# Bias features by distance, streamed both ways, and a shifted store: a bias prologue of an attention and MoE kernel

## The chip, the cores and the metric

One Trainium2 chip, one core of it. The metric is the device time of one execution in microseconds (us); lower is better. Engines are named as in the profile: PE (TensorE, matmul), PEld (its weight load), DVE (VectorE), ACT (ScalarE), POOL (GpSimd), SP (SyncE, which issues every DMA of this kernel).

## The reference, cut to what matters

Attention with a bias that a small network makes from positions, then two MoE layers. The bias depends on the row i, the column j and the head h, but not on the batch:

```python
scores = scale * np.matmul(q, k.transpose(0, 1, 3, 2))         # B=4, H=8, S=576, D=64
rel = (pos[:, None] - pos[None, :]).astype(np.float32)
psi_rel = np.log1p(np.abs(rel))
psi_i = np.log1p(np.maximum(pos[:, None].astype(np.float32), 1.0))
x = (psi_rel / psi_i)[..., None]
h = np.maximum(x @ w1 + b1, 0.0)                                # 32 hidden
bias = h @ w2                                                   # S x S x H
scores = scores + bias.transpose(2, 0, 1)[None, :, :, :]
# softmax over j, times v; then relu-max MoE (512 -> 768 -> 512), then elu MoE (512 -> 2048 -> 512)
```

Since psi_i is positive, relu(psi_rel/psi_i*w1 + b1)*psi_i = relu(psi_rel*w1 + b1*psi_i): for a row i the feature is a function of the distance |i-j| alone, plus a bias per row.

## The kernel before, in words

The program is one long list of instructions per engine. It begins with a **bias prologue** (lines 121 to 199), goes on to attention (16 units n of two heads of a batch; each unit has five steps c = 0 to 4 of 128 query rows, the last of 64), and ends with the two MoE layers, which are the greater part of the time.

The prologue makes the bias of all 576 rows for all 8 heads, 16 rows at a time, in 36 rounds A. In a round:

- **Features.** Four tiles `f_t` (a4 = 0 to 3), each 128 partitions (4 rows x 32 hidden) x 576 columns, are made from `lw`, the table of log distances times w1 (lines 153 to 167). `lw` has 1148 columns, distance 0 near column 572, and the window of a row starts 4 columns earlier for each tile. A tile is made on ACT (relu with a bias, line 162) or on DVE (maximum, line 165); a small planner chooses, by `BUSY` (what each engine has already) and `COST` (us of one tile).
- **Matmuls.** Each tile is multiplied by `w28` (32 columns) into its own 32 partitions of a PSUM buffer, in two halves of 288 columns (line 183). There are four PSUM buffers (`pb`, `pbb`).
- **Eviction.** PSUM goes to an SBUF tile `o_t` with a scale and a bias per partition: on ACT in rounds 0 to 34 (line 194), on DVE in round 35 (line 192). There are six `o_t` buffers.
- **Store.** SP stores `o_t` to the DRAM scratch `scr` (line 196). After every eighth round SP also loads the two bias tiles of the first pair of heads for chunk c from `scr` (line 109); those loads wait for that chunk's eight stores, and SP is in order, so the next stores stand behind them. Chunk 4 has four rounds and two loads of 64 rows (line 114).

Features run AH = 3 rounds ahead of the matmuls in program order; 18 feature buffers allow four and a half rounds.

Three things of the start matter too. `cst`, the bias of the eviction, needs a small matmul, a copy to `cv` and a multiply (lines 169 to 175); they stand after round 0's matmuls, and the second half of `lw` (line 174) stands there as well. `pk_t`, a pack of small tables, is the first load of SP, and the two halves of `lt_t` come behind it.

Attention's first softmax steps use `ident2`, two 64x64 identities; POOL scales it by the reciprocal row sums into `dg_t` (line 249), and PE transposes the exponentials with that (`flip`, line 252). `ident2` lies in the pool `xp`, which takes over the SBUF of the prologue's feature and `o_t` buffers; the two copies that fill it (lines 210 and 211) stand on DVE behind the first six score instructions (line 230). The score instruction of step c needs the bias tile of chunk c. With n = 0, step c = 4 is the first that needs chunk 4.

## Time and profile before

| what | value |
|---|---|
| median of 3 runs | 1009.87 us (1009.82 to 1012.12) |
| the profiled execution's own time | 1010.22 us |
| its span | 1008.4 us |
| PE busy | 977.4 us, 97% of the span |
| DVE / ACT / POOL busy | 692.1 / 526.1 / 341.7 us |
| mean granted TensorE clock | 0.997 of full speed |

The span is the profiled part of an execution; the execution's own time is 1.8 us longer. A busy share of 97% is a mean over stages: in the prologue, DVE and ACT are busy all the time too, so the stage has to be read by itself. The granted clock is 1.0 where TensorE runs at 2.4 GHz and 0.5 where it runs at 1.2 GHz; a value between them is a stretch with both.

### The profile page before, as it was taken

The page shows a single profiled execution, that of the slowest core. Times are in us where ns is not written, and L with a number is a line of the kernel's source. Part 1 is how long each engine was busy: PE and PEld are TensorE (multiplying, and loading weights), DVE is VectorE, ACT ScalarE, POOL GpSimd, SP SyncE. Part 2 cuts the span into 40 slices and gives each one's busy share as a digit, 9 for nine tenths or more (in the row PEclk, how much of TensorE's full clock was granted, in tenths as well). Part 3 has the DMA queues.
Part 4 walks back from the last instruction along what each step waited for, and adds up shares of the span by engine and source line. Part 5 has one row for each costly group of instructions (what it writes and reads, how often), then busy time and mean ns, then how long its engine had stood idle before and what let it go on. Part 6 is the DMA issues. An engine that isn't in the chain of part 4 may idle for free.

```text
span 1008.4 us, 28525 instructions
## 1 busy us (share of the span) xinstructions
PE 977.4 (97%) x11748; PEld 869.2 (86%) x11748; DVE 692.1 (69%) x1428; ACT 526.1 (52%) x1087; POOL 341.7 (34%) x419
## 2 busy tenths in 40 slices
PE   7979899999999999999999999999999999999998
PEld 4447777778887899999999999998998989988996
DVE  7967778788886699887887862835574355743342
ACT  8967777777775233333333331644445344453443
POOL 0013344344343354534553550323232132321222
PEclk9989999999999999999999999999999999999999
DMA  7842724645532356879886981355657556575553
GB/s 259 291 172 85 247 94 157 205 163 187 176 127 79 134 187 215 308 234 341 321 282 236 328 298 47 116 189 175 199 192 252 191 171 204 188 258 185 176 197 105
DMA packets 65905, 201.00 MB, mean 199 GB/s; under 512 B 7024, under 2 KB 14832, under 8 KB 65776
## 3 DMA queue, kind: packets, MB, share of 16 engines
q1 hardware_dynamic: 65776, 199.18, 57.6%
q8 instruction: 93, 1.52, 0.6%
q14 instruction: 36, 0.29, 0.1%
HBM read 150.78 MB, written 48.37 MB: 197 GB/s over the span
## 4 chain that ended last, share of the span: by engine, by line
PE 91%; DVE 6%; issue 1%; DMA 1%; ACT 0%; SPq 0%; POOL 0%; DVEq 0%; POOLq 0%; ACTq 0%
PE xo L696 18%; PE pb L740 13%; PE pb L526 12%; PE tq L740 6%; PE tq L252 6%; PE xo L319 6%; PE xo L526 5%; PE tq L526 5%; PE pb L222 5%; PE pb L620 4%; PE pb L183 3%; PE pbb L183 2%; DVE e_t L230 2%; PE xo L620 2%; PE tq L620 2%
## 5 line engine op out<-in xcount | busy, mean ns | idle before, releaser
L81 POOL TENSOR_TENSOR gl<-t_t,gh 128x384 fp32r<-128x384 f32 x96 | 108.7, 1142 | 286.3 <-ACT gh L75 286.3
L235 ACT ACTIVATE e_t<-e_t,st_t 128x576 f32<-128x576 f32 x144 | 111.4, 773 | 58.6 <-DVE st_t L240 56.1
L230 DVE CUSTOM_DVE_ANT_0 e_t<-pb,b_t 128x576 f32<-128x576 f32 x144 | 107.7, 749 | 32.7 <-PE pb L222 32.5
L249 POOL TENSOR_SCALAR dg_t<-ident,st_t 128x64 f32<-128x64 f32 x144 | 48.1, 348 | 212.7 <-DVE st_t L241 93.2
L740 PE MATMUL pb<-w_t,gh 128*128 128x512 f32 x384 | 119.3, 392 | 0.0
L526 PE MATMUL pb<-xh,w_t 128*128 128x384 f32 x448 | 116.8, 336 | 0.0
L252 PEld LDWEIGHTS tq<-dg_t,e_t 64*64 64x64 f32 x4608 | 96.6, 136 | 22.7 <-issue 7.7
L252 PE MATMUL tq<-dg_t,e_t 64*64 64x64 f32 x4608 | 97.8, 222 | 10.9 <-issue 5.3
L696 PE MATMUL xo<-tt,w_t 128*128 128x384 f32 x528 | 107.4, 338 | 0.0
L718 ACT ACTIVATE t_t<-c_t 128x384 f32<-128x384 f32 x96 | 50.0, 521 | 103.4 <-DVE c_t L709 95.6
L222 PE MATMUL pb<-kq_t 64*64 64x288 f32 x1152 | 98.6, 413 | 3.8 <-issue 1.3
L696 PEld LDWEIGHTS xo<-tt,w_t 128*128 128x128 f32 x528 | 95.0, 188 | 7.7 <-issue 0.3
L696 PE MATMUL xo<-xh,w_t 128*128 128x384 f32 x328 | 94.6, 335 | 0.0
L319 PE MATMUL xo<-p,tv_t 64*64 64x320 f32 (+1 forms) x1024 | 85.4, 408 | 1.6 <-issue 1.2
L526 PEld LDWEIGHTS pb<-xh,w_t 128*128 128x128 f32 x448 | 81.1, 188 | 0.5 <-issue 0.4
L740 PEld LDWEIGHTS pb<-w_t,gh 128*128 128x128 f32 x384 | 70.5, 188 | 6.6
L740 PE MATMUL pb<-w_t,gl 128*128 128x512 f32 x192 | 75.5, 393 | 0.0
L526 PE MATMUL pb<-xl,w_t 128*128 128x384 f32 x224 | 75.3, 336 | 0.0
L75 ACT ACTIVATE p<-tq 128x512 f32<-128x512 f32 (+1 forms) x128 | 62.8, 528 | 16.4 <-PE tq L252 15.2
L222 PEld LDWEIGHTS pb<-kq_t 64*64 64x64 f32 x1152 | 50.9, 133 | 22.9 <-DVE p L77 4.4
L75 ACT ACTIVATE gh<-t_t 128x384 fp32r<-128x384 f32 x96 | 48.6, 519 | 33.4 <-DVE t_t L726 33.4
L696 PEld LDWEIGHTS xo<-xh,w_t 128*128 128x128 f32 x328 | 60.2, 188 | 3.0
(131 smaller groups left out, 2198.1 us busy)
## 6 DMA issues: line engine op xcount, KB each, us to landing
w_t<-scw_w SPq DMA_DIRECT2D x90, 512.0 KB, 4.4
w_t<-scw_wi SPq DMA_DIRECT2D x74, 512.0 KB, 4.2
kq_t<-tkq SPq DMA_DIRECT2D x16, 864.0 KB, 5.4
scw_wi<-sp SPq DMA_DIRECT2D x26, 512.0 KB, 4.7
scw_w<-sp SPq DMA_DIRECT2D x22, 512.0 KB, 5.5
raw<-wo SPq DMA_DIRECT2D x22, 512.0 KB, 3.7
scr<-o_t SPq DMA_DIRECT2D x36, 288.0 KB, 3.9
raw<-wm SPq DMA_DIRECT2D x18, 512.0 KB, 4.1
```

Of the source, the lines that this page charges most:

```text
L75: nc.scalar.activation(dst, src, AF.Copy)
L81: e.tensor_tensor(out=dst, in0=src, in1=hi.bitcast(F32), op=ALU.subtract)
L183: mm(p[32 * a4:32 * a4 + 32, 224 + 288 * hf:512 + 288 * hf], w28, FT[A, a4][:, 288 * hf:288 * hf + 288], start=True, stop=True)
L222: mm(PB[h][H64[g], 224 + 288 * r:512 + 288 * r], t[H64[r], 576 + 576 * a + q0:640 + 576 * a + q0], t[H64[r], 288 * a:288 * a + 288], start ...
L230: nc.vector.tensor_tensor_reduce(out=E[s][:, 576 * h:576 * h + 576], in0=PB[h][:, 224:800], in1=BT[n // 4, c, h], op0=ALU.add, op1=ALU.min ...
L235: nc.scalar.activation(e, e, AF.Exp, bias=st[:, h:h + 1], scale=-1.0, accum_out=st[:, 2 + h:3 + h])
L252: mm(dst, E[s][H64[g], k0:k0 + 64], DG[s][H64[g], h % nheads(s)], start=True, stop=True)
L319: mm(XO[g][H64[h], 0:w], v[H64[g], 128 * k + 64 * h:128 * k + 64 * h + 64], ps[0][H64[g], 4 * h + k, :], start=(k == 0), stop=(k == 3 and ...
L526: mm(ps[blk][:, 0:NB], wt[:, ks], xt[:, kk, t0:t0 + NB], start=(j == 0), stop=(j == 11))
L620: mm(ps[blk][:, 0:NB], WO[0][:, kk, wt, ms], xt[:, bs], start=(j == 0), stop=(j == 3 * NM1 - 1))
L696: mm(ps, w[wt][:, ks], b[xt][:, kk], start=(start and j == 0), stop=(stop and j == 5), skip_group_check=True)
L740: mm(acc[t], g[:, ts], w[k], start=(f == 0 and i == 0 and j == 0), stop=(f == NU - 1 and i == 1 and j == 2))
```

## The change

- **Features by distance.** `lw` shrinks to 576 columns, one for each distance 0 to 575. A round's features cover only the distances that its 16 rows reach, n = max(576-16A, 16A+16): 576 in round 0, 304 in rounds 17 and 18, 576 again in round 35.
- **Two directions.** The matmuls read a feature tile forwards for the columns j >= i, and backwards (step -1) for those below. A round's PSUM now has 591 columns, the same for all its 16 rows, as if all had the row 16A: two groups of four matmuls in most rounds, three in the first four and the last four, where a PSUM bank's limit splits one direction.
- **Shift on the way to DRAM.** Row i of the 16 is to lie i columns further. The scratch gets rows of 608 floats and the store goes to a start that moves by one float per row, 591 floats of each, so the loads find column 0 at float 16.
- **Order.** The small matmul for `cv` comes ahead of the features; `cv` and `cst` follow round 0's features on DVE. `lt_t` is loaded first, in one piece, then `pk_t`. `ident2` moves to the pool `const` and is filled at the start.
- **Planner.** `BUSY` and `COST` change; `COST` is now a constant and a part for the width. It gives DVE 119 features (51,760 columns, mean 435) and ACT 25 (11,600 columns, mean 464).

```diff
@@ -28,6 +28,7 @@
 NU = NF // 2
 NB = 384
 BIG = 3.0e38
+SW = 608
 
 
 
@@ -45,8 +46,8 @@
 
 EV = "a" * 35 + "v"
 AH = 3
-BUSY = {"v": 4.0, "a": 0.3, "p": 0.0}
-COST = {"v": 0.43, "a": 0.67}
+BUSY = {"v": 0.9, "a": 0.0, "p": 0.0}
+COST = {"v": (0.06, 0.37), "a": (0.26, 0.42)}
 EVC = {"v": 0.80, "a": 0.74}
 
 
@@ -63,10 +64,14 @@
 
     ident = const.tile([128, 128], F32, name="ident")
     make_identity(nc, ident)
+    ident2 = const.tile([128, 64], F32, name="ident2")
     rebias = const.tile([128, 1], F32, name="rebias")
     nc.vector.memset(rebias, -896.0 * 2.0 ** 23)
 
-    scr = [dram.tile([128 if c < 4 else 64, H, S], F32, name=f"scr{c}") for c in range(5)]
+    scr = [dram.tile([(128 if c < 4 else 64) * (H * SW + 1)], F32, name=f"scr{c}") for c in range(5)]
+
+    def rows(c, i0, n):
+        return scr[c][i0 * H * SW:(i0 + n) * H * SW]
 
     def hi_of(eng, dst, src):
         if eng == "p":
@@ -105,13 +110,14 @@
         if c < 4:
             for h in range(2):
                 t = bp.tile([128, 576], F32, tag="b", name="b_t")
-                src = scr[c][:, 2 * hp + h, :]
+                src = rows(c, 0, 128).rearrange("(i h j) -> i h j", h=H, j=SW)[:, 2 * hp + h, 16:592]
                 nc.sync.dma_start(t, src)
                 BT[hp, c, h] = t
         else:
             t = bp.tile([128, 576], F32, tag="b", name="b_t")
             for h in range(2):
-                nc.sync.dma_start(t[64 * h:64 * h + 64], scr[4][:, 2 * hp + h, :])
+                src = rows(4, 0, 64).rearrange("(i h j) -> i h j", h=H, j=SW)[:, 2 * hp + h, 16:592]
+                nc.sync.dma_start(t[64 * h:64 * h + 64], src)
             BT[hp, 4, 0] = t
 
     pab = ctx.enter_context(tc.tile_pool(name="pab", bufs=1, space=PSUM))
@@ -125,39 +131,41 @@
         fp = pro.enter_context(tc.tile_pool(name="fp", bufs=18, side="right"))
         bt = pro.enter_context(tc.tile_pool(name="bt", bufs=6, side="right"))
 
-        lt_t = pc.tile([128, 1148], F32, name="lt_t")
+        lt_t = pc.tile([128, 576], F32, name="lt_t")
         pk_t = pc.tile([128, 230], F32, name="pk_t")
         w1_t, b1_t = pk_t[:, 0:1], pk_t[:, 1:2]
         w2_t, psi_t = pk_t[:, 2:34], pk_t[:, 34:178]
         mk_t, ip_t = pk_t[:, 178:194], pk_t[:, 194:230]
         w28 = pc.tile([128, 32], F32, name="w28")
-        lw = pc.tile([128, 1148], F32, name="lw")
+        lw = pc.tile([128, 576], F32, name="lw")
         pbt = pc.tile([128, 144], F32, name="pbt")
         nbt = pc.tile([128, 144], F32, name="nbt")
         cst = pc.tile([128, 16], F32, name="cst")
         cv = pc.tile([128, 1], F32, name="cv")
 
         with tc.manual_schedule():
+            nc.sync.dma_start(lt_t, lt)
             nc.sync.dma_start(pk_t, pk)
-            nc.sync.dma_start(lt_t[:, 512:1148], lt[:, 512:1148])
-            nc.sync.dma_start(lt_t[:, 0:512], lt[:, 0:512])
             load_kq(0)
             load_v(0)
+            for r in (slice(0, 64), slice(64, 128)):
+                nc.vector.tensor_copy(ident2[r], ident[r, r])
             nc.vector.tensor_scalar(nbt, psi_t, b1_t, -1.0, op0=ALU.mult, op1=ALU.mult)
             nc.vector.tensor_scalar(pbt, psi_t, b1_t, None, op0=ALU.mult)
-            nc.vector.tensor_scalar(lw[:, 512:1148], lt_t[:, 512:1148], w1_t, None, op0=ALU.mult)
+            nc.vector.tensor_scalar(lw, lt_t, w1_t, None, op0=ALU.mult)
             nc.gpsimd.tensor_scalar(w28, w2_t, 8.0, 1.0, op0=ALU.mult, op1=ALU.mult)
             busy, cost = dict(BUSY), COST
             FT, PAT = {}, {}
 
             def feat(A):
-                pat = 0
+                pat, n = 0, max(S - 16 * A, 16 * A + 16)
+                share = n / S
                 for a4 in range(4):
                     a = 4 * A + a4
-                    f = FT[A, a4] = fp.tile([128, 576], F32, tag="f", name="f_t")
-                    win = lw[:, 572 - 4 * a:572 - 4 * a + 576]
-                    e = min(cost, key=lambda x: busy[x] + cost[x])
-                    busy[e] += cost[e]
+                    f = FT[A, a4] = fp.tile([128, 576], F32, tag="f", name="f_t")[:, 0:n]
+                    win = lw[:, 0:n]
+                    e = min(cost, key=lambda x: busy[x] + cost[x][0] + cost[x][1] * share)
+                    busy[e] += cost[e][0] + cost[e][1] * share
                     if e == "a":
                         nc.scalar.activation(f, win, AF.Relu, bias=pbt[:, a:a + 1])
                         pat |= 1 << a4
@@ -166,34 +174,38 @@
                 PAT[A] = pat
                 busy[EV[A]] += EVC[EV[A]]
 
-            def consts(p):
-                for a4 in range(4):
-                    mm(p[32 * a4:32 * a4 + 32, 0:1], w28, b1_t, start=True, stop=True)
-                nc.vector.tensor_copy(cv, p[:, 0:1])
-                nc.vector.tensor_scalar(cst, mk_t, cv, None, op0=ALU.mult)
-                nc.vector.tensor_scalar(lw[:, 0:512], lt_t[:, 0:512], w1_t, None, op0=ALU.mult)
-                busy["v"] += 0.7
-
+            for a4 in range(4):
+                mm(PBB[3][32 * a4:32 * a4 + 32, 0:1], w28, b1_t, start=True, stop=True)
             for A in range(AH):
                 feat(A)
+                if A == 0:
+                    nc.vector.tensor_copy(cv, PBB[3][:, 0:1])
+                    nc.vector.tensor_scalar(cst, mk_t, cv, None, op0=ALU.mult)
             for A in range(36):
                 p = PBB[A % 4]
-                for hf in range(2):
+                back, fore = 16 * A + 15, S - 16 * A
+                c0 = 224 if fore > 512 else 800 if back > 512 else 512
+                near = 288 if fore > 512 else fore
+                far = 288 if back > 512 else back
+                parts = [(c0, 0, near, 1), (c0 - far, far, far, -1)]
+                parts += [(512, 288, fore - 288, 1)] if fore > 512 else [(c0 - back, back, back - 288, -1)] if back > 512 else []
+                for col, d0, n, sgn in parts:
                     for a4 in range(4):
-                        mm(p[32 * a4:32 * a4 + 32, 224 + 288 * hf:512 + 288 * hf], w28,
-                           FT[A, a4][:, 288 * hf:288 * hf + 288], start=True, stop=True)
-                if A == 0:
-                    consts(p)
+                        f = FT[A, a4][:, d0:d0 + n] if sgn > 0 else FT[A, a4][:, d0 - n + 1:d0 + 1][:, ::-1]
+                        mm(p[32 * a4:32 * a4 + 32, col:col + n], w28, f, start=True, stop=True)
+                pv_ = p[:, c0 - back:c0 + fore]
                 if A + AH < 36:
                     feat(A + AH)
-                o = bt.tile([128, 576], F32, tag="o", name="o_t")
+                o = bt.tile([128, 591], F32, tag="o", name="o_t")
                 j = PAT[A]
                 if EV[A] == "v":
-                    nc.vector.tensor_scalar(o, p[:, 224:800], ip_t[:, A:A + 1], cst[:, j:j + 1], op0=ALU.mult, op1=ALU.add)
+                    nc.vector.tensor_scalar(o, pv_, ip_t[:, A:A + 1], cst[:, j:j + 1], op0=ALU.mult, op1=ALU.add)
                 else:
-                    nc.scalar.activation(o, p[:, 224:800], AF.Identity, bias=cst[:, j:j + 1], scale=ip_t[:, A:A + 1])
+                    nc.scalar.activation(o, pv_, AF.Identity, bias=cst[:, j:j + 1], scale=ip_t[:, A:A + 1])
                 c, r = divmod(A, 8)
-                nc.sync.dma_start(scr[c].rearrange("i h j -> (i h) j")[128 * r:128 * r + 128, :], o)
+                b0 = 16 * r * H * SW + 1
+                dst = scr[c][b0:b0 + 16 * (H * SW + 1)].rearrange("(i x) -> i x", i=16)[:, 0:H * SW]
+                nc.sync.dma_start(dst.rearrange("i (h j) -> i h j", j=SW)[:, :, 0:591], o)
                 if A % 8 == 7:
                     load_b(0, c)
             load_b(0, 4)
@@ -206,9 +218,6 @@
     psp = ctx.enter_context(tc.tile_pool(name="psp", bufs=1, space=PSUM))
     TQ, XO = [[psp.tile([128, 512], F32, name=f"{n}{i}") for i in range(2)] for n in ("tq", "xo")]
     PAIR = [(PB[i][:, 0:512], PB[i][:, 512:1024]) for i in (1, 0)] + [tuple(TQ), tuple(XO)]
-    ident2 = xp.tile([128, 64], F32, name="ident2")
-    nc.vector.tensor_copy(ident2[0:64], ident[0:64, 0:64])
-    nc.vector.tensor_copy(ident2[64:128], ident[64:128, 64:128])
     H64 = [slice(0, 64), slice(64, 128)]
     steps = [(n, c) for n in range(4 * NP) for c in range(5)]
     E, ST, PT = {}, {}, {}
@@ -860,8 +869,7 @@
     vv[:, 0:64, 576:640] = vp[:, 1, 512:]
 
     g = np.repeat(np.arange(4), HID)
-    m = np.arange(1148)
-    lt = np.log1p(np.abs(m[None, :] - 572 - g[:, None]).astype(f)).astype(f)
+    lt = np.repeat(np.log1p(np.arange(S).astype(f))[None, :], 128, axis=0).astype(f)
     i = 4 * np.arange(144)[None, :] + g[:, None]
     psi = np.log1p(np.maximum(i.astype(f), f(1.0))).astype(f)
     i = 16 * np.arange(36)[None, :] + np.repeat(np.arange(16), 8)[:, None]
```

What now stands where on two places of DVE:

DVE at the start of the prologue, before (`lw` is the table that all features read, `cst` the eviction's bias):

```order
L67 MEMSET rebias 128x1
L146 TENSOR_SCALAR nbt<-pk_t 128x144
L147 TENSOR_SCALAR pbt<-pk_t 128x144
L148 TENSOR_SCALAR lw<-lt_t,pk_t 128x636
L165 TENSOR_SCALAR f_t<-lw,nbt 128x576 x5
L172 COPY cv<-pb_99 128x1
L173 TENSOR_SCALAR cst<-pk_t,cv 128x16
L174 TENSOR_SCALAR lw<-lt_t,pk_t 128x512
L165 TENSOR_SCALAR f_t<-lw,nbt 128x576 x102
L192 TENSOR_SCALAR o_t<-pbb_108,pk_t,cst 128x576
```

The same place with the change, as far as round 4's features:

```order
L69 MEMSET rebias 128x1
L152 COPY ident_71<-ident 64x64 x2
L153 TENSOR_SCALAR nbt<-pk_t 128x144
L154 TENSOR_SCALAR pbt<-pk_t 128x144
L155 TENSOR_SCALAR lw<-lt_t,pk_t 128x576
L173 TENSOR_SCALAR f_t<-lw,nbt 128x576 x2
L182 COPY cv<-pbb_109 128x1
L183 TENSOR_SCALAR cst<-pk_t,cv 128x16
L173 TENSOR_SCALAR f_t<-lw,nbt 128x560 x3
L173 TENSOR_SCALAR f_t<-lw,nbt 128x544 x3
L173 TENSOR_SCALAR f_t<-lw,nbt 128x528 x3
L173 TENSOR_SCALAR f_t<-lw,nbt 128x512 x3
```

The copy of `cv` moved from behind five features and round 0's matmuls to behind two features, the second piece of `lw` is gone, and the widths fall round by round.

DVE at the passage to attention, before (`e_t` are the scores, `st_t` their row statistics, `ident_863` is `ident2`, `p` what PE transposed):

```order
L230 ISA e_t,st_t<-pb_100,b_t 128x576
L230 ISA st_t 128x1
L230 ISA e_t,st_t<-pb_99,b_t 128x576
L230 ISA st_t 128x1
L240 TENSOR_SCALAR st_t<-st_t 128x2
L241 RECIPROCAL st_t<-st_t 128x2
L230 ISA e_t,st_t<-pb_100,b_t 128x576
L230 ISA st_t 128x1
L210 COPY ident_863<-ident 64x64
L211 COPY ident_863<-ident 64x64
L77 COPY p_921<-pb_99 128x128
L77 COPY p_920<-tq_860 128x8x64
```

The same place with the change:

```order
L239 ISA e_t,st_t<-pb_101,b_t 128x576
L239 ISA st_t 128x1
L239 ISA e_t,st_t<-pb_100,b_t 128x576
L239 ISA st_t 128x1
L249 TENSOR_SCALAR st_t<-st_t 128x2
L250 RECIPROCAL st_t<-st_t 128x2
L239 ISA e_t,st_t<-pb_101,b_t 128x576
L239 ISA st_t 128x1
L82 COPY p_951<-pb_100 128x128
L82 COPY p_950<-tq_893 128x8x64
```

The two identity copies are gone from between the scores and the copies of transposed tiles; the rest keeps its order.

## Rows read from the trace of the kernel before

**Rows 1.** The page's chain that ended last, shares of the span by engine.
```profile
PE 91%; DVE 6%; issue 1%; DMA 1%; ACT 0%; SPq 0%; POOL 0%; DVEq 0%; POOLq 0%; ACTq 0%
```

**Rows 2.** Windows: length, busy us (instructions) of each engine, PE clock, DMA share, GB/s.
```profile
24.00:36.00 12.00, 12.00 (x148) 5.46 (x146) 12.00 (x29) 12.00 (x18) 0.00 (x0) 1.00 0.78 274
...
60.00:66.00 6.00, 2.66 (x80) 2.15 (x80) 2.43 (x10) 1.73 (x6) 1.18 (x4) 0.76 0.50 169
66.00:72.00 6.00, 5.17 (x144) 3.73 (x140) 3.26 (x10) 3.85 (x8) 0.60 (x2) 0.67 0.01 3
```

**Rows 3.** Groups by line and form, 5 to 57 us: busy us, mean ns, idle before.
```profile
L165 DVE TENSOR_SCALAR f_t<-lw,nbt 128x576 f32<-128x576 f32 x107 | 46.1, 509 | 0.0
...
L162 ACT ACTIVATE f_t<-lw,pbt 128x576 f32<-128x576 f32 x37 | 28.8, 797 | 3.0 <-DVE lw L148 3.0
...
L148 DVE TENSOR_SCALAR lw<-lt_t,pk_t 128x636 f32<-128x636 f32 x1 | 0.6, 551 | 1.1 <-DMA lt_t<-lt 1.1
...
L174 DVE TENSOR_SCALAR lw<-lt_t,pk_t 128x512 f32<-128x512 f32 x1 | 0.5, 481 | 0.0
```

**Rows 4.** Timeline, 0 to 20 us: start, us for the whole piece, engine, line.
```profile
5.06 5.44 ACT L162 ACTIVATE f_t<-lw,pbt 128x576 f32<-128x576 f32 x8 [3.04 <-DVE lw L148]
...
10.12 0.16 DVE L172 COPY cv<-pb 128x1 f32<-128x1 f32 x1 [2.83 <-PE pb L171]
...
10.86 9.53 DVE L165 TENSOR_SCALAR f_t<-lw,nbt 128x576 f32<-128x576 f32 x22
```

**Rows 5.** Chain in order of time, 0 to 100 us: start, us, what.
```profile
12.04 1.70 PE pbb L183 x28
...
13.98 1.79 PE pb L183 x28
...
54.71 0.98 ACT o_t L194 x2
```

**Rows 6.** Timeline of SP, then of ACT, at the third chunk boundary.
```profile
42.08 0.32 SPq L196 DMA_DIRECT2D scr<-o_t  x1
...
50.64 0.83 ACT L194 ACTIVATE o_t<-pbb,cst,pk_t 128x576 f32<-128x576 f32 x1 [0.27 <-DMA scr<-o_t]
```

**Rows 7.** DMA issues, 0 to 70 us: count, KB each, median us to landing.
```profile
b_t<-scr SPq DMA_DIRECT2D x8, 288.0 KB, 3.3
...
lt_t<-lt SPq DMA_DIRECT2D x1, 318.0 KB, 3.3
b_t<-scr SPq DMA_DIRECT2D x2, 144.0 KB, 2.8
...
pk_t<-pk SPq DMA_DIRECT2D x1, 115.0 KB, 2.1
```

**Rows 8.** Chain in order of time, 56 to 76 us, the passage to attention.
```profile
58.77 3.58 DMA scr<-o_t
...
62.96 0.19 DVE ident L210
...
64.06 1.99 PE tq L252 x64
...
70.53 0.30 DVE p L77
...
71.59 1.07 PE tq L252 x64
...
75.36 0.12 PE pb L252 x8
```

**Rows 9.** Timeline, 48 to 78 us: reciprocal, queries, chunk 4's load, chunk 4's first score.
```profile
59.50 0.17 DVE L241 RECIPROCAL st_t<-st_t 128x2 f32<-128x2 f32 x1
...
60.38 0.71 PE L222 MATMUL pb<-kq_t 64*64 64x288 f32 x8 [0.40 <-DVE st_t L230]
...
62.66 1.15 SPq L114 DMA_DIRECT2D b_t<-scr  x2
...
71.66 0.76 DVE L230 CUSTOM_DVE_ANT_0 e_t<-pb,b_t 128x576 f32<-128x576 f32 x1 [0.84 <-PE pb L222]
```

## The prediction

> **What bounds the kernel now.** I read the chain first: 91% of it is PE [rows 1], so whatever comes before attention delays the whole rest, and a microsecond taken from the prologue is a microsecond of the kernel, unless a later wait takes it back. Then the windows: between 24 and 36 us PE, DVE and ACT are all busy for the full 12 us and DMA for 0.78 of it [rows 2]; four things are close together, and the busy share does not say which leads. The groups settle part of that: DVE makes 107 features and has no idle time before them, ACT makes 37 [rows 3]. DVE's pace is 9.53 us for 22, 0.433 us each; ACT's 5.44 for 8, 0.68 [rows 4]. From ACT's first feature at 5.06 to the end of its last eviction at 54.71 + 0.98 = 55.69 [rows 4, 5] it did 37 features and 35 evictions with one wait of 0.27 [rows 6], so an eviction costs (50.63 - 0.27 - 37 x 0.68)/35 = 0.72 us. PE isn't the bound: while it catches up on work that lies ready, its chain goes from 12.04 to 13.98 for two rounds, 0.97 us a round [rows 5], against 1.30 for the three features that DVE makes in one. So DVE and ACT, balanced, set the prologue's length.
>
> After 60 us the picture is another one. PE is busy 2.66 of 6 us, and its granted clock falls to a mean of 0.76, then 0.67 [rows 2]: some of that time at 1.2 GHz instead of 2.4, after PE had waited. The chain there says why: DVE's identity copies start at 62.96, behind the landing of the last stores (58.77 + 3.58), and PE's transposes at 64.06 [rows 8].
>
> **The features.** DVE now makes 119, of 435 columns on average. What does a column cost? One row pair shows it for this operation and engine: 636 columns 551 ns, 512 columns 481 [rows 3], 0.565 ns a column. A mean feature is then 0.433 - 141 x 0.000565 = 0.353 us, and 119 make 42.0. The bounds: if width cost nothing, 51.5, which the row pair speaks against; if time went by width alone, 38.9. ACT: 25 features of 464 columns by the same slope 0.617 each, 15.4, and 35 evictions with 15 more columns, 25.5: together 40.9. If ACT's time did not fall with width it would be 42.5, if it fell with width alone 39.2. DVE remains the bound, by a little. PE with 591 columns instead of 576 needs 0.97 x 591/576 = 1.00 us a round, 36 us in all: covered, but in the middle rounds, where 3.3 features of 304 columns cost DVE 0.92, PE leads by some hundredths; the buffers of a round and a half take that up.
>
> **The constants.** Before, DVE waited 2.83 us for the small matmul behind round 0 and then spent 10.86 - 10.12 = 0.74 on three operations [rows 4]. Now the matmul comes first, so I cost its wait at nothing, and two operations remain, 0.4. DVE's stretch was 107 x 0.433 + 2.83 + 0.74 = 49.9; it becomes 42.4. The swap of the first loads: a table of 318 KB took 3.3 us to land, the pack 2.1 [rows 7]; now both must be there before the first `lw`, and two small multiplies stand between. I take 0.2 later (0 to 0.4). The identity copies at the front are covered by these loads. So the last eviction would come 7.5 - 0.2 = 7.3 us earlier.
>
> **What is late next: the `o_t` buffers.** At a chunk boundary SP waits for the stores, issues two loads, and only then the next chunk's stores. At the third boundary the eighth store was issued at 42.08, and the eviction that needed the next store's buffer could start at 50.64: a turn of 8.6 us, with a wait of 0.27 [rows 6]. Seven rounds fit between: 7 x 1.29 - 0.72 = 8.3, where 1.29 is 36 rounds' mean. With the change the same seven rounds take, at 3.3 features of 408, 325 and 440 columns, periods of 1.12, 1.00 (PE) and 1.18: 7.1, 6.3 and 7.5 us. Against a turn of 8.6 that makes waits of 1.5, 2.3 and 1.1 at the three boundaries, 4.9 in all. That is the upper bound, since at the first two boundaries before nothing waited, so their turns may be shorter; the lower one is 0. I take 2.8, nearer the upper end, because the only turn that shows itself is the long one. ACT, which has little slack, pays it in full. The prologue so gains 7.3 - 2.8 = 4.5 us.
>
> **The shifted store.** It moves 2.6% more bytes, to starts that are no multiple of the row. No store of before does that. The nearest rows are loads: `lt_t` takes pieces of a wider table, 318 KB in 3.3 us, no slower than 288 KB of whole rows [rows 7]. I take 0 beside the bytes, and a store 1.3 times as long as the other end. The Trainium skill (DMA: Bandwidth & Descriptors, How a descriptor splits into AXI transactions) says that a descriptor which doesn't start on 256 bytes begins its first transaction below its start and pays for the unused part; an estimate from it is 78 beats of 32 bytes for a row instead of 72. By that each turn would be some 0.3 us longer, and the time about 1002; the loads here don't show it, and no row shows it for stores.
>
> **The passage to attention.** With `ident2` ready from the start, POOL can scale it once the reciprocals are done (59.50 + 0.17), and PE's transposes come after the sixth group of query matmuls, which ends at 60.38 + 0.71 = 61.09 [rows 9], instead of 64.06: 3.0 us. And PE then has no wait of three microseconds, after which the clock fell. The sequence transposes, copy, queries, transposes, ending ahead of the next copy, ran from 64.06 to 70.53, 6.5 us, and the same one from 71.59 to 75.48 at full clock, 3.9 us [rows 2, 8]: 2.6 us more at most, if the clock holds. DVE's scores and copies stand between, so I take 1.5, and 4.5 for the passage; the bounds are 3.0 and 5.6. What is late next is chunk 4's bias: its second load was issued about 0.6 after 62.66 and needs 2.8 [rows 7, 9], so it lands at 66.1; its score ran at 71.66 and may move 4.5, not more than 5.6. Stores and loads shift with the last eviction, so this slack holds.
>
> **The sum.** The profiled execution took 1010.22 us (span 1008.4 and 1.8 around it), 0.35 above the median of the runs. 1010.2 - 4.5 - 4.5 = **1001.2 us**. The ends of its own terms: -7.3 and -5.6 give 997.3; -2.4 and -3.0 give 1004.8.
>
> **Rivals.**
>
> - **Backward reading is slow, and PE becomes the bound.** No row shows a moving operand with step -1. A round reads 288 columns forwards and 303 backwards; at 0.97/576 = 1.68 ns a column that is 0.485 + 0.51 f us for a factor f. PE starts at about 6 us and has 0.9 us behind it, so 36 rounds end later than 55.69 + 4.5, and the kernel is slower, from f = 1.95. At f = 2.5 the rounds take 63.4 us, the last eviction comes at 70.3, and the time is 1010.2 + 14.6 - 4.5 = **1020**. For it: the transposes and queries all read forwards, so nothing excludes it. Against: PE has room, since it leads DVE's mean round of 3.3 x 0.353 = 1.17 us only from f = 1.35. Chance 0.10.
> - **Shifted stores are slow, and DMA becomes the bound.** At 0.78 busy [rows 2], 15% faster rounds with 2.6% more bytes ask for 0.92. A store 1.3 times as long goes beyond 1: I estimate that the turns lengthen to over 10 us; waits of about 3, 4 and 3 use up the 7.3 and more, the last eviction comes 2 to 3 us later than before, and chunk 4 delays its score. What is left is the passage, 3 at best: **1008 to 1010**. For it: the step of one float. Against: the `lt_t` row. Chance 0.11.
> - **The features do not get faster than the evictions allow.** ACT waits at the start for a PE that is still slow, and the turns cost their 4.9 us: only the passage remains, with 0 to 1.5 us of the prologue: **1004 to 1006**. Chance 0.10.
> - **No turn waits and the clock holds:** under **997.5**. Chance 0.05.
>
> **How the numbers follow.** The forecast's case has 0.64. The range reaches from 997.5 to 1008, which leaves out the backward case, the better case and some of the store's case, together about 0.2. A measurement of this kernel can tell about 0.3%, 3 us. Faster: 0.64, the third and fourth rival, and a little of the store's, 0.80. Same: most of the store's, 0.09. Slower: the backward case and a worse store, 0.11.
>
> **What would show it.** DVE's 119 features should take about 42 us with hardly an idle gap, and its copy of `cv` should not wait. ACT should show waits for stores at two or three evictions, 2 to 3 us in all; if none, the time is below 1000. The last eviction on ACT should end near 51. PE's backward matmuls should start as far apart as forward ones of their width; if they don't, I am wrong from there. A store should land in about 4 us as before. The transposes should start near 57, with the clock at full between 55 and 65; the score of chunk 4 should come near 62.7 and wait for PE, not for DMA.

## The result, and the profile after

The change makes the kernel slower: 1018.0 us, the median of 10 runs (1015.04 to 1022.42), against 1010.76 (10 runs, 1009.57 to 1015.37) on the same chip; ratio 1.007 [1.005, 1.0091]. The forecast was 1001.2, with 997.5 to 1008 as the range. The profiled execution took 1017.18 us (span 1015.4), 7.0 more than before.

The engines did what the forecast says. Timeline of DVE, then of ACT, of the changed kernel, at the start (start, us, engine, line):

```profile
4.39 0.52 DVE L155 TENSOR_SCALAR lw<-lt_t,pk_t 128x576 f32<-128x576 f32 x1
...
5.80 0.15 DVE L182 COPY cv<-pbb 128x1 f32<-128x1 f32 x1
...
6.13 34.57 DVE L173 TENSOR_SCALAR f_t<-lw,nbt 128x560 f32<-128x560 f32 x100
...
4.94 3.36 ACT L170 ACTIVATE f_t<-lw,pbt 128x576 f32<-128x576 f32 x5 [2.92 <-DVE lw L155]
```

DVE makes a hundred features in 34.57 us without a gap, 0.346 each. They have 414 columns in the mean, and the forecast's slope gives 0.341 for that width. Its copy of `cv` waits for nothing, where it waited 2.83 us [rows 4]. ACT's first feature starts at 4.94 instead of 5.06.

Timeline of PE, 28 to 33 us:

```profile
29.56 2.41 PE L195 MATMUL pb<-f_t,w 128*32 128x256 f32 x32
31.55 1.84 PE L195 MATMUL pbb<-f_t,w 128*32 128x224 f32 x26
```

Thirty-two matmuls, two rounds with half of their columns read backwards, take 1.99 us from the first start of one group to that of the next: 1.0 a round, as for forward reading at full clock [rows 5].

And yet ACT's last eviction ends no sooner than before. Evictions on ACT that wait for a store, from its timeline, and the last one:

```profile
26.47 0.84 ACT L204 ACTIVATE o_t<-pbb,cst,pk_t 128x591 f32<-128x591 f32 x1 [2.50 <-DMA scr<-o_t]
38.60 0.84 ACT L204 ACTIVATE o_t<-pbb,cst,pk_t 128x591 f32<-128x591 f32 x1 [4.08 <-DMA scr<-o_t]
50.62 1.74 ACT L204 ACTIVATE o_t<-pbb,cst,pk_t 128x591 f32<-128x591 f32 x2 [1.89 <-DMA scr<-o_t]
54.15 0.84 ACT L204 ACTIVATE o_t<-pb,cst,pk_t 128x591 f32<-128x591 f32 x1 [0.40 <-DMA scr<-o_t]
54.92 0.84 ACT L204 ACTIVATE o_t<-pbb,cst,pk_t 128x591 f32<-128x591 f32 x1
```

The three boundaries cost 2.5, 4.1 and 2.3 us, 8.9 in all, where 1.5, 2.3 and 1.1 were worked out and 2.8 taken. The last eviction ends at 55.76 (55.69 before [rows 5]). SP at the first of these boundaries, from its timeline:

```profile
17.60 0.52 SPq L208 DMA_DIRECT2D scr<-o_t  x1
21.00 0.81 SPq L114 DMA_DIRECT2D b_t<-scr  x2
21.86 0.53 SPq L208 DMA_DIRECT2D scr<-o_t  x1
```

The chunk's eighth store is issued at 17.60 and lands 3.3 us later; only then come the two loads, and the next chunk's first store at 21.86. The eviction that needs that store's buffer starts at 26.47: a turn of 8.9 us. At the three boundaries the eighth store landed 3.3, 4.6 and 4.8 us after its issue (before: 2.2, 2.6 and 2.2), SP issued the next store after 4.3, 5.4 and 5.8 us (before: 3.2, 3.5 and 3.3), and the turns were 8.9, 10.1 and 9.9 us.

The chain of waits of the changed kernel, in order of time (start, us, what):

```profile
21.86 4.51 DMA scr<-o_t
...
28.52 4.57 DMA scr<-o_t
...
33.95 4.55 DMA scr<-o_t
...
48.40 5.64 DMA scr<-o_t
...
60.42 5.57 DMA scr<-o_t
...
66.66 4.35 DMA b_t<-scr
...
71.16 0.76 DVE e_t L239
```

Before, the prologue's chain was PE's rounds [rows 5]. Now stores stand between the rounds, and behind the last of them the load of chunk 4's bias: its score starts at 71.16 instead of 71.66 [rows 9]. DVE waits 4.65 us for that load. Windows of the changed kernel answer to [rows 2]:

```profile
24.00:36.00 12.00, 12.00 (x177) 7.27 (x172) 12.00 (x39) 8.01 (x12) 0.00 (x0) 1.00 0.78 251
...
60.00:66.00 6.00, 4.15 (x168) 3.34 (x168) 4.33 (x16) 4.33 (x10) 1.33 (x5) 1.00 0.69 228
66.00:72.00 6.00, 1.84 (x86) 1.39 (x76) 1.13 (x4) 1.35 (x3) 0.00 (x0) 1.00 0.72 236
```

ACT falls from 12.0 busy us to 8.0 in the first, and DMA is 0.78 busy in both kernels: there it is not full, it is waited for. (From 48 to 54 us it is full, 0.99, against 0.90 before.) In 60 to 66 PE gains what `ident2` was to bring (2.66 to 4.15); in 66 to 72 it waits for chunk 4 most of the time (5.17 to 1.84).

SP shows why. What the DMA queue of SP waited for, 20 to 72 us, before:

```profile
SPq L109 <- DMA scr<-o_t: 7.9, 6, 2.0
...
SPq L114 <- DMA scr<-o_t: 2.9, 2, 2.3
```

and in the changed kernel (L114 and L120 are the same two lines there):

```profile
SPq L114 <- DMA scr<-o_t: 12.8, 8, 4.2
SPq L120 <- DMA scr<-o_t: 4.4, 1, 4.4
```

In front of bias loads SP waits 17.2 us for stores to land, instead of 10.8. All that time it can issue no store.

**A second loss lies where the change touches nothing.** The score at 82.33 us, the fifteenth, is level with before's:

```profile
82.33 0.75 DVE L239 CUSTOM_DVE_ANT_0 e_t<-pb,b_t 128x576 f32<-128x576 f32 x1
...
321.01 0.74 DVE L239 CUSTOM_DVE_ANT_0 e_t<-pb,b_t 128x576 f32<-128x576 f32 x1
```

(the second is the last score but one). The same two instructions before:

```profile
82.50 0.74 DVE L230 CUSTOM_DVE_ANT_0 e_t<-pb,b_t 128x576 f32<-128x576 f32 x1
...
313.96 0.74 DVE L230 CUSTOM_DVE_ANT_0 e_t<-pb,b_t 128x576 f32<-128x576 f32 x1
```

So the prologue and the passage together brought 0.2 us instead of 9.0, and attention, from 82 to 321 us, lost 7.2. Together these 8.8 and 7.2 us are the 16.0 between the forecast, 1001.2, and the profiled execution, 1017.18. Windows from the fifteenth score to the last but one, and three others of the changed kernel:

```profile
82.33:321.01 238.68, 221.26 (x6721) 184.84 (x6717) 193.76 (x588) 175.97 (x422) 96.46 (x197) 0.99 0.45 153
260.00:280.00 20.00, 17.36 (x496) 13.99 (x491) 14.47 (x45) 13.07 (x33) 7.15 (x15) 0.95 0.44 156
280.00:300.00 20.00, 19.88 (x604) 17.11 (x598) 15.83 (x51) 15.71 (x38) 8.07 (x17) 0.96 0.34 117
178.23:181.23 3.00, 3.00 (x100) 2.55 (x96) 1.13 (x4) 1.80 (x5) 0.00 (x0) 1.00 0.96 312
```

The first of them before:

```profile
82.50:313.96 231.46, 218.12 (x6721) 182.12 (x6717) 193.99 (x588) 176.21 (x422) 96.00 (x197) 1.00 0.46 158
```

PE is idle for 17.4 us instead of 13.3, and busy 3.1 us longer for the same 6,721 matmuls. Of these 3.1 some 1.8 are the clock (an estimate: 0.05 and 0.04 of 20 us each): behind a gap of 1.99 us, which ends at 277.11, the granted clock falls for a stretch to 1.2 GHz, as it did nowhere in this part before.

What PE waited for there, 82 to 300 us, in the changed kernel:

```profile
PE tq L261 <- issue: 6.5, 7, 1.8
PE xo L328 <- issue: 4.0, 4, 2.0
PE pb L231 <- issue: 2.5, 3, 1.4
```

and before:

```profile
PE tq L252 <- issue: 5.3, 7, 1.7
...
PE pb L252 <- issue: 1.7, 2, 1.2
PE pb L222 <- issue: 1.3, 1, 1.3
PE xo L319 <- issue: 0.5, 1, 0.5
```

"Issue" is idle time in which the engine waited for nothing that the profile shows: 13.0 us against 8.8. The trace's packet records tell more: of the 11 gaps of over 0.6 us in the changed kernel 10 end 1.2 to 1.7 us behind the end of a 16 KB instruction packet, and 6 of the 7 before 1.2 to 1.8 behind one. PE seems to wait for its code; no run changed the packets alone, so this is read from times that fall together.

The packets ahead of the gaps were not slow but late. In the changed kernel nine gaps put down to "issue" stand behind a packet; these packets took 0.95 us (median; the other 39 of 82 to 300 us: 1.09), but each began 5.6 us behind the one before it instead of 4.2, and in the 3 us before they began DMA was 0.93 busy in the mean, instead of 0.41. The window at 178.23 above is such a case: the packet began at 181.23. In the traces of all twenty kernels, none of the 321 packets that began with DMA under 0.2 busy has such a gap behind it; of the 186 that began with DMA over 0.9 busy, 41% have one.

### The profile page after: what moved, and what is told of

The parts are those of the page before. It is cut to its first block, busy times and chain, and to the rows that moved or that the text cites. A ratio compares the mean times of both kernels' runs of the same rounds, so it can differ in the third digit from the quotient of the medians.

```text
span 1015.4 us, 28658 instructions
## 1 busy us (share of the span) xinstructions
PE 973.0 (96%) x11812; PEld 873.3 (86%) x11812; DVE 687.3 (68%) x1439; ACT 517.6 (51%) x1075; POOL 342.7 (34%) x419
## 4 chain that ended last, share of the span: by engine, by line
PE 88%; DVE 5%; DMA 4%; issue 2%; ACT 1%; SPq 0%; POOL 0%; DVEq 0%; ACTq 0%; POOLq 0%
PE xo L705 18%; PE pb L749 13%; PE pb L535 12%; PE tq L749 6%; PE xo L328 6%; PE tq L261 6%; PE xo L535 5%; PE tq L535 5%; PE pb L231 5%; PE pb L629 4%; DMA scr<-o_t 2%; PE xo L629 2%; PE tq L629 2%; DVE e_t L239 2%; PE pb L261 1%
## 5 line engine op out<-in xcount | busy, mean ns | idle before, releaser
L80 ACT ACTIVATE gh<-t_t 128x384 fp32r<-128x384 f32 x96 | 48.5, 519 | 33.4 <-DVE t_t L735 33.4
```

What stands on the lines that cost most here:

```text
L80: nc.scalar.activation(dst, src, AF.Copy)
```

## The experiments

Each time is the median of a kernel's runs, each ratio stands against the kernel before on the same chip. "Level at the 15th score" compares that score's start with 82.50 us of before; "attention" is what is lost from there to the last score but one. Both come from one profiled execution each, and executions of one kernel lie up to 13 us apart: those of x4 (1003.01, median 1007.05), w1 (1010.39, 1006.8) and y4 (1020.95, 1016.88) stand 3.6 to 4.1 us off their medians, so a difference of some us between two kernels in these two numbers shows nothing by itself.

### Is it the shifted store? x1, x2, x3, y3, y4

x1 stores and loads rows of equal pitch, without the shift (its rows follow each other evenly, and it is issued in 0.32 us like x2's 128 plain rows). x2 does so from a start one float off. x3 stores plain rows and shifts in the load, by a pitch one float shorter, so that the same bias comes out.

```diff
# x1
+                dst = rows(c, 16 * r, 16).rearrange("(i h j) -> i h j", h=H, j=SW)
+                nc.sync.dma_start(dst[:, :, 0:591], o)
# x2
+                dst = scr[c][b0:b0 + 128 * SW].rearrange("(p j) -> p j", j=SW)
+                nc.sync.dma_start(dst[:, 0:591], o)
# x3: x2's store from b0 = 16 * r * (H * SW - 1), and in the load
+        return scr[c][15:15 + n * (H * SW - 1)].rearrange("(i x) -> i x", i=n)[:, h * SW:h * SW + S]
```

> The change without the shift: the store keeps its shape of 16 rows of 8 runs (pitch 608 floats, 591 of each), but every run starts at a multiple of 64 bytes and the rows don't move (so the bias columns are not aligned row by row: the output is another one). Theory ODD (what costs is that the shifted store starts off any boundary): stores land in about 3.9 us again, the waits of ACT for stores fall from 9 us to 3 or less, the time is 1001 to 1004. Theory SHAPE (what costs is the split of a 16 x 8 store over the DMA engines, whatever its start): as the change, 1015 to 1019, waits of 7 us or more, issue 0.5 us a store.

> The change with the store written as 128 equal rows (pitch 608 floats, 591 of each), all starting one float behind a 64-byte boundary; rows don't move, so the output is another one. Theory ODD: as the change, 1013 to 1019, landing about 4.6 us. Theory SHAPE: 1001 to 1004, landing about 3.9 us and issue 0.32 us a store, as before.

> The change with the shift moved from the stores to the loads: the store is 128 equal rows on 64-byte starts, and the load's row pitch is one float shorter than the store's, so the loads start off boundaries. The output is the same as the change's. ODD and SHAPE both expect the stores to land in about 3.9 us and the time at 1001 to 1004, unless odd starts cost loads as well: then the loads (3.0 to 3.3 us) grow by a third and the time is 1004 to 1010.

Measured: 1012.93, 1012.8 and 1012.83 us, ratios 1.0025 [1.0002, 1.0048], 1.0026 [1.0008, 1.0044] and 1.0013 [0.9993, 1.0034]. ACT still waits 5.6 to 7.0 us for stores, and DVE 4.2 to 4.4 for chunk 4. So with plain stores the kernel is some 5 us faster, and still slower than before: the store is not the main cause. The odd start is no part of it: the packets of x2 took 98.1 ns in the mean, those of x1 and x3 98.1 and 98.0, and those of the change 114.0. y3 makes the pitch 609, so that each row starts at another place, and y4 is the change's 16 x 8 form with all starts aligned (a pitch of 4880 floats per 8 rows); neither shifts.

```diff
# y3
-SW = 608
+SW = 609
# y4
+    RP = H * SW + 16
+        v = scr[c][i0 * RP:(i0 + n) * RP].rearrange("(i x) -> i x", i=n)[:, 0:H * SW]
+        return v.rearrange("i (h j) -> i h j", j=SW)
...
+                nc.sync.dma_start(rows(c, 16 * r, 16)[:, :, 0:591], o)
```

> x2 with a row pitch of 609 floats instead of 608: 128 equal rows in one flat store, but each row starts 4 bytes further on from the 64-byte boundary than the row before (the output is another one). Theory STARTS (rows whose starts differ in alignment slow the packets): mean packet of a store 110 ns or more, time as the change, 1014 to 1019. Theory SHAPE (the 16 x 8 form, which x1's equal pitches folded into 128 rows, is what slows them): 98 ns, issue 0.32 us, 1010 to 1014 as x1 to x3.

> The change's store as a true 16 x 8 x 591, with a pitch of 4880 floats between the 16 rows, which does not fold into 128 rows, and every run on a 64-byte start (the output is another one). SHAPE: mean packet 110 ns or more, issue about 0.52 us, 1014 to 1019. STARTS: 98 ns and 1010 to 1014, whatever the issue takes.

Measured: y3 1013.58, ratio 1.0037 [1.0015, 1.006], packets 99.6 ns; y4 1016.88, 1.0049 [1.0014, 1.0085], packets 117.5 ns. It is the **form**, not the alignment, that slows the packets in the mean (the median is 95 ns in all of them). What that costs is less plain: at the 15th score y4 stands 4.6 us behind x1, but the change is level with x3 (82.33 and 82.38); the 3.0 us between their profiled executions lie in attention (table below). With plain stores, too, SP's turn grows: in x3 it issued the next chunk's first store 5.0, 5.5 and 5.6 us after the eighth store. SP's issues of the store, min/median/max in ns, in y3:

```profile
L208 SPq DMA_DIRECT2D scr<-o_t x36: 319/432/1325, 9.5 to 61.3; - x36
```

and in y4:

```profile
L209 SPq DMA_DIRECT2D scr<-o_t x36: 517/597/1446, 9.6 to 63.1; - x36
```

A destination of 16 x 8 rows that can't be read as 128 plain ones takes at least 0.52 us to issue instead of 0.32 (median 0.60 instead of 0.43). The Trainium skill (DMA: Bandwidth & Descriptors, How a descriptor splits into AXI transactions) has a descriptor that starts off 256 bytes pay for more beats. These runs neither show nor exclude it: rows of 608 floats are 2,432 bytes, so at least half of x1's starts lie off 256 bytes too; an estimate from that count gives x2 as many beats as x1, and y3 up to 3% more, where its packets took 1.5% longer.

### ident2 alone: x4

The kernel before, with `ident2` made first, and nothing else of the change.

> The kernel before with one part of the change alone: the two identity copies at the start, in a pool of their own. If the passage to attention is worth what was forecast: 1005 to 1007, transposes at about 61 instead of 64 and the clock at full from 60 to 72 us. Rival: chunk 4's load ends last there, and the gain is 2 us or less.

Measured: 1007.05 us, ratio 0.9963 [0.994, 0.9986]. The ratio is worth 3.7 us, between 1.4 and 6.1; the profiled execution, the fastest of the seven, is ahead 5.2 us at the 15th score (the passage's term: 4.5, bounds 3.0 and 5.6), and its granted clock is 1.00 from 56 to 76 us. Its chain at the passage:

```profile
59.22 4.78 DMA scr<-o_t
...
64.64 2.99 DMA b_t<-scr
...
67.79 0.76 DVE e_t L230
```

Chunk 4's score comes 3.9 us earlier and waits for its load, which was not the chain's before [rows 8].

### Is it the buffers, or SP's order? y1, y2, z1, z2, z3, w1, w2

y2 is the change with the bias loads of a chunk issued four rounds later, when that chunk's stores have landed; y1 does the same to x3, z1 to x4, and z3 is y2 with `ident2` where it was.

```diff
-                if A % 8 == 7:
-                    load_b(0, c)
+                if A in (11, 19, 27):
+                    load_b(0, c - 1)
+            load_b(0, 3)
```

> x3 (flat stores on 64-byte starts, shift on the load) with one more edit: a chunk's two bias loads stand four rounds later on SP, behind stores that can go at once, so that SP doesn't wait for landings at a chunk boundary; chunk 3's loads stand behind the last store. Theory TURN (what eats the prologue's gain is SP's wait at the boundary, which keeps the six o_t buffers from coming free): ACT's waits for stores fall from 7 us to 1 or less, its last eviction ends at 49 to 50 instead of 55.9, the time is 1000 to 1003. Rival THROUGHPUT (the faster rounds ask for more than DMA moves): waits of 4 us or more stay, now spread over the rounds, the last eviction ends after 52, the time is 1006 or more.

> The change as it is (shifted 16 x 8 stores) with the same later loads as y1. TURN alone would make it as fast as y1. If the shifted stores cost DMA time of their own (packets of 114 ns in the mean instead of 98), 36 stores and the loads ask for about all of DMA, waits of 2 to 4 us stay, the last eviction ends at 51 to 53, the time is 1004 to 1009.

> The kernel before with the identity copies first (x4) and the bias loads four rounds later (as y1 and y2), without anything else of the change. If the later loads give nothing where no turn is too long (before, ACT waited 0.27 us for a store), this is x4 again at its best, 1003 to 1006, and what lies between it and y2 (about 1000) is what the features by distance give: 4 to 6 us. Rival: the later loads by themselves make the gain of y2, and this runs at 1000 as well.

> y2 with the identity copies back behind the release of the prologue's buffers, as in the kernel before. What the identity's move is worth where the turn is mended: 3 to 4.5 us by the forecast, so 1002.5 to 1005, with transposes again behind the landing of the last store; if chunk 4's load ends last in the passage anyway, 1.5 us or less.

Measured: y1 1001.33, 0.9916 [0.9892, 0.994]; **y2 999.71**, 0.9908 [0.9876, 0.994]; z1 1003.48, 0.9944 [0.9919, 0.9969]; z3 1003.06, 0.9927 [0.9905, 0.9949]. One edit takes 17.7 us from the changed kernel's profiled execution, 12.5 of them ahead of the 15th score and 5.2 in attention. SP's waits for landings, 20 to 72 us, in y2:

```profile
SPq L120 <- DMA scr<-o_t: 1.5, 2, 0.8
SPq L114 <- DMA scr<-o_t: 1.0, 2, 0.7
```

17.2 us have become 2.5. y2 keeps the slow form of the store, and is no slower than y1 without it. z1 says what the rest of the change is worth there: with the later loads and `ident2` first, but the old features, constants and stores, it stands 5.9 us behind y2 at the 15th score, so the later loads do not make y2's gain alone. z3, y2 with `ident2` where it was, stands 1.4 us behind y2 there, and 3.4 in the medians, which are of two chips. In y2 ACT waits 1.4 us for stores, and the last eviction on ACT ends at 49.46. The windows of y2 show DMA full at last, and ACT busy for 10.6 and 11.0 of 12 us:

```profile
24.00:36.00 12.00, 12.00 (x182) 8.15 (x175) 12.00 (x39) 10.59 (x17) 0.00 (x0) 1.00 1.00 319
36.00:48.00 12.00, 11.63 (x185) 6.88 (x182) 11.60 (x30) 11.00 (x18) 0.00 (x0) 1.00 0.97 328
```

In z2 the loads stay in place and twelve `o_t` buffers replace six:

```diff
-        bt = pro.enter_context(tc.tile_pool(name="bt", bufs=6, side="right"))
+        bt = pro.enter_context(tc.tile_pool(name="bt", bufs=12, side="right"))
```

> The change with twelve o_t buffers instead of six, and the loads where the change has them. TURN: the wait goes with the buffers as it went with the later loads; ACT's waits for stores fall below 1 us and its last eviction ends at 49 to 50. SP still waits at each boundary, so the last stores and chunk 4's loads come later than in y2, and chunk 4's score waits for them: 1002 to 1008. Rival: if SP's blocked time rather than the buffers is what counts, ACT ends early and the time stays at 1012 or more.

Measured: 1014.42 us, 1.0048 [1.0029, 1.0067]. ACT waits for no store and its last eviction ends at 48.6. The chain of z2:

```profile
52.09 3.88 DMA scr<-o_t
...
56.26 2.78 DMA b_t<-scr
...
59.27 5.58 DMA scr<-o_t
...
65.52 2.76 DMA b_t<-scr
...
68.45 0.76 DVE e_t L239
```

All evictions are done seven microseconds earlier, and chunk 4's score comes 2.7 earlier. The evictions didn't hold the stores; SP did: it still waits 15.9 us in front of bias loads (11.7 and 4.2).

w1 is the change with the loads of chunks 0 to 3 in their old place, but issued by POOL; w2 is y1 with ten buffers.

```diff
-                    load_b(0, c)
+                    load_b(0, c, nc.gpsimd)
```

> The change as it is, with one edit: the bias loads of chunks 0 to 3 keep their place in the program but are issued by POOL instead of SP, so SP goes on to the next chunk's stores while the loads wait for the landings. The later loads brought 1018 to 999.7; they did two things at once, took the waits out of SP's order and moved the loads' traffic. If SP's order is what costs, this gives the same: the last eviction on ACT ends near 49 to 50, ACT waits under 2 us for stores, and the time is 999 to 1003. If the early place of the loads costs, through the traffic that they take from the stores, the last eviction stays at 53 to 55, ACT still waits 5 us or more, and the time stays at 1012 to 1018.

> The flat aligned stores with the shift in the loads, later loads, and ten o_t buffers instead of six. If the evictions still stood behind stores with six buffers, the last one comes a little sooner and the time is 997 to 999. If the features' pace alone sets the last eviction there (48.5 us, no waits for stores), nothing changes: 999 to 1002.5. A time over 1005 would mean that more stores in flight hold up the loads of chunk 4.

Measured: w1 1006.8, 0.9961 [0.9935, 0.9986]; w2 1000.41, 0.9905 [0.9875, 0.9935]. Off SP's queue, the loads' early place no longer holds up ACT: no wait for a store, last eviction done at 48.5, and at the 15th score w1 is 8.7 us ahead. So SP's order is what costs. That the time stayed above what was expected goes with the loss in attention (8.9 us, below, in an execution 3.6 us above the median), and with POOL's queue, in its timeline:

```profile
23.86 27.66 POOL L114 DMA_DIRECT2D b_t<-scr  x8 [19.60 <-DMA scr<-o_t]
```

The first of the eight issues took 23.88 us, to 47.74; DVE had made features without a gap from 21.90 to 47.61. So chunk 0's bias landed at 52.0, and the first score came 2.4 us later than in y2. The Trainium skill (SBUF — State Buffer, SBUF: two separate sides) says that POOL can't write the descriptors of its DMAs while VectorE, in an operation that takes two ports, holds the pair of ports that they share. The trace agrees: the first issue ended 0.1 us behind the last feature. That these features take two ports no row tells. w2 equals y1, so the buffers hold nothing any more.

### What is lost in attention: p1 to p4, r1

| kernel | level at the 15th score | attention | PE idle, issue, 82 to 300 us |
|---|---|---|---|
| before | 0 | 0 | 8.8 |
| x4, z1 (old matmul order) | -5.2, -6.7 | -2.0, -0.3 | 5.9, 8.3 |
| the change | -0.2 | +7.2 | 13.0 |
| x1, x2, x3 | -2.5, -1.9, -0.1 | +4.3, +4.4, +4.2 | 10.8, 13.2, 12.6 |
| y3, y4 | +0.1, +2.1 | +3.4, +8.6 | 12.0, 16.2 |
| z2, w1 | -2.8, -8.7 | +4.7, +8.9 | 12.3, 14.5 |
| y1, z3 | -13.4, -11.2 | +4.6, +4.2 | 12.5, 11.5 |
| y2, w2 | -12.6, -12.6 | +2.0, +2.0 | 9.8, 9.9 |

The loss goes with PE's idle time without a cause, though not in step. The change adds 64 matmuls ahead of attention, 128 instructions with their weight loads, about half of a 16 KB packet (an estimate: the trace of before has 93 such packets to 23,833 records of PE, 256 each). p1 puts as many at the start of the kernel before, p2 at that of the change (a whole packet more in all); p3 and p4 add 64 and 32 to w2.

```diff
+            for _ in range(64):
+                mm(PBB[2][0:32, 0:1], ident[:, 0:32], ident[:, 0:1], start=True, stop=True)
```

> The kernel before with 64 one-column matmuls (128 instructions of PE with their weight loads, as many as the change adds ahead of attention) put at the very start, where PE waits for its first feature anyway. They touch nothing else. In the changed kernel the score after unit 2 comes at the same time as before (82.32 against 82.50 us), and the whole 7 us go between 82 and 314 us, where PE is idle 13.0 us with nothing to wait for, against 8.8; these gaps end 1.2 to 1.7 us behind a 16 KB instruction packet, the size of 256 instructions. If the place of attention's code in those packets counts, this kernel loses what the change lost: that idle time rises from 8.8 to 12 to 14 us, and the time is 1014 to 1018. If it is the traffic of the bias rows, or anything else of the change, nothing happens: 1009.5 to 1012.

> The changed kernel with the same 64 matmuls at the start, so that attention's code stands 256 instructions later than in the kernel before, one whole packet. If the place in the packets counts, attention goes as before again: idle time with nothing to wait for 6 to 9.5 us instead of 13.0, and a time of 1010 to 1014. If not, 1016 to 1020. Should a pad at the start disturb the prologue, the first score shows it; it stands at 56.58 us now.

> The version with later loads and ten o_t buffers, and the 64 matmuls at the start. Its idle time with nothing to wait for was 9.9 us, against 8.8 of before and 13.0 of the change. If the place in the packets counts alone, it comes near before's 8.8 or the 5.9 of the kernel before with ident2 first, and the time is 996 to 999.5. If the traffic at that moment decides, it can go either way by a few us: 997 to 1004.

> The same with 32 matmuls, a quarter of a packet. Neither theory gives a sign: by the place in the packets it is another phase, with an idle time between 6 and 16 us and so 996 to 1006; if place doesn't count it is as the version without a pad, 998.5 to 1002.

Measured: p1 1011.3, 0.9997 [0.9977, 1.0016], attention +0.6, idle 7.7; p2 1016.38, 1.007 [1.0028, 1.0112], +5.5, 14.0; p3 1004.83, 0.9936 [0.9912, 0.9959], +6.4, 12.9; **p4 999.26**, 0.9887 [0.9863, 0.9911], -0.3, 8.1. The theory that the place of PE's code in the packets decides **falls**: p1 has the change's place and loses nothing, p2 has before's and loses 5.5. (The pad is not free: it puts the first score of p2 at 60.18 instead of 56.58 us, and that of p3 at 52.62 instead of 49.79, where p1's comes at 57.20 instead of 56.84.) p3's loss and p4's gain were not foretold by it either.

r1 is the kernel before with the change's scratch of 608 floats a row, which attention's bias loads read:

```diff
+                src = rows(c, 0, 128).rearrange("(i h j) -> i h j", h=H, j=SW)[:, 2 * hp + h, 16:592]
...
+                nc.sync.dma_start(rows(c, 16 * r, 16).rearrange("(x j) -> x j", j=SW)[:, 16:592], o)
```

> The kernel before with one part of the change, the scratch's rows of 608 floats instead of 576: each row's 576 floats are stored and loaded at float 16 of its 608, with no shift, and every instruction of PE, DVE and ACT is as before. The 128 PE instructions alone cost the old kernel nothing (64 added matmuls: 1011.3), so what the changed kernel loses in attention must come from another part. If it is the layout that attention's bias loads read, this kernel is level with the one before at 82 us, PE is idle with nothing to wait for 11 to 14 us between 82 and 300 us instead of 8.8, and the time is 1013 to 1017. If the layout has no part in it, the idle time is 6 to 9 us, as in the other three kernels with the old layout, and the time is 1009 to 1012.

Measured: 1012.47, 1.0006 [0.9994, 1.0019], level at the 15th score (+0.1), attention +1.2, idle 8.2. The layout alone is not it. What makes PE's code late in the changed kernel **stays open**. Five kernels with the old matmul order, before among them, lie between -2.0 and +1.2, fifteen with the new one between -0.3 and +8.9; neither the number of PE's instructions, nor the place of `ident2` (x4, z1), nor the layout does it alone. Nor does the number of packets that fall due behind a busy DMA: 17 began with DMA over 0.8 busy in the changed kernel and 17 before. A candidate is how much code PE still has when such a packet is late; no run set that by itself. The code of ACT and DVE, combinations, and attention's own transfers were not tried.

## Why the prediction was wrong

- **Features, constants, PE's round, the start: right.** DVE's pace was 0.346 (0.341 by the forecast's slope for that width), the wait for `cv` went, and ACT starts 0.12 earlier rather than 0.2 later. Where nothing blocks the stores, the last eviction on ACT ends at 48.5 to 48.6 (z2, w1), 7.1 us before 55.69: the term was 7.3.
- **Backward reading is slow** (1020): the right sign for another reason. PE took 1.0 us a round.
- **The turn of the `o_t` buffers: mis-sized.** The three waits were 8.9 us, beyond the upper bound of 4.9. The turn of 8.6 us was read in a kernel whose evictions came slowly. With faster ones it was 8.9, 10.1 and 9.9 us, since the eighth store of a chunk lands later behind the seven others (3.3 to 4.8 us instead of 2.2 to 2.6) and SP waits for it: the turn grows as the rounds shrink. It grows with plain stores too (x3), so the store's form is not what it needs.
- **The shifted store at 0: too low.** Its packets were 16% slower (114.0 to 98.1 ns) and its issue 1.6 times as long, by the form of the destination. Without it the kernel takes 1012.8 (x2, x3), though ahead of attention that is worth 0 to 4.6 us, and nothing that shows once SP's order is mended (y2). The rival had slow stores at 1008 to 1010; its waits of 3, 4 and 3 us came nearly so, but DMA was not the bound: 0.78 busy from 24 to 36 us, where the rival counted on 0.92 and more.
- **"Stores and loads shift with the last eviction, so this slack holds": the step that failed.** Chunk 4's bias follows SP's queue of stores and loads, not the eviction. z2 shows it alone: evictions 7 us earlier, the load 2.7. The passage's 4.5 fits what x4 shows (5.2 in its profiled execution, 1.4 to 6.1 by its runs), and in the changed kernel the seventh score does come 4.8 us earlier (63.13 instead of 67.97); then chunk 4 takes it back. Together the two steps cost 8.8 of the 9.0 us at the 15th score. y2, where SP no longer waits in front of the loads, is 12.6 us ahead there.
- **Attention after the passage as before: put at nothing without a reason, and 7.2 us off.** No term or rival spoke of it. PE was idle there for 4.1 us more, and busy 3.1 us more for the same matmuls, some 1.8 of it by the clock. Why the idle time grew stays open. Without this loss the changed kernel would be level with the one before; the steps above are why it isn't faster.
- **Features no faster than the evictions allow** (1004 to 1006): not so at the start, where ACT's evictions don't wait; its turns of 4.9 us came, and more.
- **No turn waits gives under 997.5:** false. z2 has none and takes 1014.4.

## What to carry to other kernels

When the engines of a stage get faster, work out anew the queue that issues its transfers, instruction by instruction: an in-order queue which waits for landings before it loads becomes the bound while DMA is a fifth idle (0.78 busy from 24 to 36 us here). Put a load that depends on stores some steps behind them, so that its wait is over when the queue comes to it; here that one edit turned 1018.0 into 999.7 us, below both kernels (each beside the kernel before on its own chip: 7.2 us above it, and 11.4 below). And compare a fixed instruction before and after, stage by stage: a total can hide a gain here and a loss where nothing was edited.

## What was not expected of the hardware

- A store to 16 x 8 rows that don't fold into plain ones: packets 114 to 118 ns in the mean instead of 98 to 100, issue at least 0.52 us instead of 0.32.
- A start one float off cost these stores nothing (x2: 98.1 ns against 98.1 and 98.0 in x1 and x3), and a step of one float more between rows hardly anything (y3: 99.6).
- A load issued by POOL stood 23.9 us at the queue beside DVE's features.
- From 82 to 300 us PE lost 6 to 16 us in idle time that the profile puts to nothing; its long gaps nearly all end just behind a 16 KB instruction packet, one that began late while DMA was busy (0.93 in the mean in the changed kernel). The amount changes by several us with edits elsewhere in the program.
